# New due-date shifts and load lags in the list scheduler of a fused pooled-attention and MLP kernel

## The chip, the cores and the metric

The kernel runs on one core of a Trainium2 chip. The metric is the device time of one execution in microseconds (us), as the median of several runs; lower is better.

## The reference

`q`, `k` and `v` have 8 batches, 8 heads, 576 tokens and 64 columns per head, in float32. Keys and values are summed over windows of 8 tokens first, so 576 queries meet 72 keys.

```python
k_p = k.reshape(B, H, Sp, pool, D).mean(axis=3)
v_p = v.reshape(B, H, Sp, pool, D).mean(axis=3)
scores = scale * np.matmul(q, k_p.transpose(0, 1, 3, 2))
attn = softmax(scores)            # exp(scores - max) / sum
x = matmul(attn, v_p)             # -> 4608 tokens x 512
h = x @ w_in                      # 512 -> 2048
g = h * (1.0 / (1.0 + np.exp(-1.702 * h)))
out = g @ w_out                   # 2048 -> 512
```

## The kernel before

**Stages.** The weights `w_in` and `w_out` are loaded once, decoded and kept on the chip as a high and a low part, so that one product becomes three matmuls of the fast 32-bit format: high x high, low x high, high x low. The 512 first tokens of each attention batch form one batch of the MLP (c = 0 to 7), and the 64 left-over tokens of all eight form the last one (c = 8). The attention of batch b runs on the other engines while TensorE (PE) does the products of the MLP batch before it. One batch of the MLP takes about 96 us of PE, and some 85 us pass at the start until the first weights are decoded and the first attention is done.

**Products.** Batches 0 and 1 do `x @ w_in` directly (function `dense`: line 1217 and the two behind it for h, 1259 to 1261 for o). From batch 2 on, two of the sixteen 128-wide blocks of the hidden width are a pair p (0 to 7), whose 2x2x2 blocks are done in seven products instead of eight, by sums of blocks of x and of the weights made ahead (function `pair`). A product is six matmuls of 256 columns at L1421. Four products of a pair go to a PSUM bank ha and three to a bank hb. Each product of ha is copied out by `keep` (L1436, ScalarE = ACT or VectorE = DVE) before the next may be added to the same bank; `plus` (L1443, DVE) adds hb to a copied part. Pair p+1 takes the two banks that pair p leaves, so its first product waits for the last copy of ha. After a part is complete comes the gelu (L1460 and L1468 on ACT, the difference at L1475 on GpSimd = POOL or DVE), which gives the operands ghall and glall of the second product: groups of three matmuls of 512 columns (L1622 to L1624), eight groups for each pair, into four accumulators oC_0, oC_128, oC_256 and oC_384 of batch C. A complete accumulator is copied by ACT to a staging buffer osb with two places and stored from there (L1172; the third copy of a batch waits for the first one's store, the fourth for the second one's).

**The attention beside it.** For batch B, SP's queue loads keys and values in two halves (kvB_u_False the keys, kvB_u_True the values; function `fetch_main`, issued at L470, two DMAs of 128 KB for each half), queries in pieces (qr, L522, four DMAs a piece) and the tails of 64 tokens (tl). DVE sums the windows (L553: redB_v0 and redB_v1 are the values, red_k the keys; L563 spreads them with a mask), turns the queries (L740), takes the maximum of the scores sps (L779, L787), and after the exponentials on ACT (L799) the sum, the inverse and the product (L804, L816, L817, L822 on sm and sc), and copies the weights of the attention to main and tail (L851, L861, DVE or ACT). Scores are matmuls at L756; the transposes of the weights at L880 (apt) and the product with the values at L958 (pav) are PE's too. In the batches up to 2, main and tail are written by L822 directly. The first operands of a pair of batch C come back from DRAM through SP: wsC_p_0 to wsC_p_2 (512 KB each) and the last one in a place named shared (256 KB; L1354, function `fetch_pair`).

**What sets the order.** The program is written down as tasks, and a list scheduler, class `Plan`, decides in which order each engine gets its instructions. A task has a kind, made of the engine, what it writes and its batch and part ("DVE red2_0", "PE o1_128"), and a due time: where none is given, it is worked back from the tasks that need it, as their due time less SLACK times (duration + lag). Then SHIFTS adds a number for the task's kind. `wait` tells how long after a task another may begin that needs it: for a DMA its lag (2.2 us unless LAGS gives another), 0.25 or 1.2 us for PE, else 0.2. `order` goes through a modelled time and gives each engine that is free the ready task with the earliest due time. The instructions are emitted in the order so planned. On the chip each engine works through its own list in that order, and waits for semaphores where an operand is late; modelled times don't delay anything there. DMAs are issued by SP in list order too, so a DMA that waits for its buffer holds up those behind it. The operands of a pair go to the places of the pair two before it: the load of shared for pair 2 waits for the last product of pair 0 that reads it, ha5_0's fourth, and that of ws5_3_1 for hb5_1's second product.

Of the kernel before, what the change touches and what calls it, by code (L numbers as in the profile page):

```python
# [19 lines left out]
POOL = 8  # L20
# [4 lines left out]
EAGER = 50.0  # L25
UNTIL = 58.0
WARM = 222.0
SLACK = 1.5
BLOCKED = 20.0

LAGS = {"kv": 3.2, "tl": 3.0, "qr": 2.5}

SHIFTS = {
    "ACT g0_256": 14, "ACT g1_0": 8, "ACT gh0_0": -4, "ACT gh0_256": -8, "ACT gh1_0": -33, "ACT osb0_128": 17,
    "ACT qt0_1": 2, "ACT stage": 13, "ACT vh0": 6, "ACT x0_0": 12, "ACT x1_0": 18, "ACT x2_0": -18, "DMA qr2_0": -12,
# [5 lines left out]
    "POOL raw": 18, "POOL stage": 2, "POOL stage0_2": -22, "POOL stage0_6": -9, "POOL stage0_7": -49,  # L43
}


# [22 lines left out]

class Task:  # L70
    __slots__ = "engine us emit due after before bufs ready left begun table k port other mode kind lag".split()


class Plan:
# [54 lines left out]
    @staticmethod  # L129
    def wait(a, b):  # L130

        if a.engine == b.engine and a.engine != "DMA":
            return 0.0
        if a.engine == "DMA":
            return a.lag
        if b.engine == "OUT":
            return 2.2
        if b.engine == "PE":
            return 0.25 if b.due < 150 else 1.2
        return 0.2  # L140

    def room(self, t, wanted):
        need = {}
# [12 lines left out]
    def order(self):  # L156
# [2 lines left out]
            if t.due is None:  # L159
                t.due = min([o.due - SLACK * (t.us + self.wait(t, o)) for o in t.after] + [LATEST])  # L160
        for t in self.tasks:
            t.due += SHIFTS.get(t.kind, 0.0)
        free = dict.fromkeys(ENGINES, 0.0)
        free["DMA"] = 2.0
        port = {"DVE": 0.0, "POOL": 0.0}
# [24 lines left out]
        while len(placed) < len(self.tasks) or running:  # L190
            for end, k, t in sorted(running):
                if end > now + 1e-9:
                    break
                running.remove((end, k, t))
                for b in t.bufs:
                    b.users -= 1
                    if not b.users and b.ring is not None:
                        b.ring.room += 1
                for o in t.after:
                    o.left -= 1  # L200
                    o.ready = max(o.ready, end + self.wait(t, o))
                    if not o.left:
                        offer(o)
            for e in ENGINES:
                if free[e] > now + 1e-9:
                    continue
                rival = {"DVE": "POOL", "POOL": "DVE"}.get(e)
                blocked = rival is not None and port[rival] > now
                best = None
                for t in ready[e]:  # L210
                    if t.ready > now + 1e-9 or e != t.engine and now < t.due:
                        continue
                    rank = (t.due + (BLOCKED if blocked and t.port and e == "DVE" else 0.0), t.k)
                    if (best is None or rank < best[0]) and self.room(t, wanted):
                        best = rank, t
                if best is None:
                    continue
                t = best[1]
                ready[t.engine].remove(t)
                us = t.us  # L220
                if t.other is not None:
                    ready[t.other[0]].remove(t)
                    if e != t.engine:
                        t.engine, us, t.emit, t.port = t.other
                if t.table not in (None, table):
                    table, us = t.table, us + 1.28
                if e == "PE":
                    if now < COLD:
                        us *= 2.0
                    elif t.mode != mode:  # L230
                        us += 0.08
                    mode = t.mode
                if e == "DMA" and now < 16:
                    us *= 1.25
                if t.port:
                    if blocked:
                        us += port[rival] - now
                    port[e] = now + us
                for b in t.bufs:
                    if b.ring is not None and not b.held:  # L240
                        b.held = True
                        b.ring.room -= 1
                        if b.ring.fifo:
                            b.ring.queue.pop(0)
                t.begun, t.us, free[e] = now, us, now + us
                running.append((now + us, t.k, t))
                placed.append(t)
            times = [end for end, _, _ in running]
            times += [f for f in free.values() if f > now + 1e-9]
            times += [t.ready for e in ENGINES for t in ready[e] if t.ready > now + 1e-9]  # L250
            times += [t.due for e in ENGINES for t in ready[e] if t.other is not None and t.due > now + 1e-9]
            if not times:
                if len(placed) < len(self.tasks):
                    raise RuntimeError(f"stuck at {now}")
                break
            now = min(times)
# [4 lines left out]
def attention_moe_kernel(ctx: ExitStack, tc: tile.TileContext, q, k, v, w_in, w_out, out):  # L261
# [1081 lines left out]
    def fetch_pair(c, p):  # L1343

        got = []
        for k in range(4):
            if k < 3:
                b, also = home(2 * W_PLACES[p % 2][k], [P, 2, 512], F32R, f"ws{c}_{p}_{k}"), []
            else:
                b, whole = share(LAST_PLACE, [P, 2, 2, 256], F32R, p % 2, f"ws{c}_{p}_{k}")  # L1350
                also = [whole]
            t = dma(
                P * (4096 if k < 3 else 2048),
                lambda b=b, k=k: nc.sync.dma_start(out=b().bitcast(F32), in_=w_dram[p][k]),  # L1354
                [w_refs[p][k]],
                [b],
            )
            hold(t, *also)
            got.append(b)

        def op(k, half):
            cols = slice(256 * half, 256 * half + 256)
            return got[k], lambda: got[k]()[:, :, cols].rearrange("p r (j c) -> p r j c", j=2)

        return {"11": op(0, 0), "12": op(0, 1), "s3": op(1, 0), "s1": op(1, 1), "s2": op(2, 0), "s4": op(2, 1), "22": op(3, 0)}
# [191 lines left out]
    for b in range(1, B):  # L1557
# [17 lines left out]
        if b == FROM - 1:  # L1575
            stage = quarters([P, 2, CHUNK], F32, "stage")
# [108 lines left out]
```

## Time and profile before

| | |
|---|---|
| median of three runs | 930.7 us (928.47, 930.70, 934.69) |
| the profiled execution | 930.27 us |
| its span, first to last instruction | 928.2 us |
| PE busy with matmuls | 908.7 us, 98% |
| PE's weight loads | 813.3 us, 88% |
| DVE / ACT / POOL busy | 71% / 59% / 34% |
| granted clock of PE | 1.00 |

A row of a timeline gives start, length, engine, line, operation, what is written and read, and in brackets the idle time before it and who ended that. Batch and buffer numbers are left out of the names there. A row of waits gives who waited for whom, and then the sum, the number and the longest. DVE and ACT are idle for large parts, but they work in order, so a late operand of one instruction delays all that is behind it.

### The profile page before, as it was taken

To read this page: it belongs to the slowest core of one execution; us is meant where nothing else is said; L and a number is where in the kernel's file an instruction comes from. 1 tells how busy PE (TensorE), PEld (TensorE's weight loads), DVE (VectorE), ACT (ScalarE), POOL (GpSimd) and SP (SyncE) were. 2 spreads that over 40 slices of the span, in tenths; PEclk is the share of its full clock that TensorE was granted. 3 is DMA by queue.
4 is the path that set the end of the run, shared out by engine and by line. 5 is a ranking of instruction groups with operands and counts; after the bars stand their busy time and mean duration, and the time that the engine had idled before them with its cause. 6 is when DMAs were issued, how large, how long until landed. Compare 5 with 4: busy or idle time off the path is not lost.

```text
span 928.2 us, 16289 instructions
## 1 busy us (share of the span) xinstructions
PE 908.7 (98%) x5689; PEld 813.3 (88%) x5689; DVE 657.4 (71%) x1232; ACT 545.5 (59%) x1211; POOL 318.8 (34%) x306
## 2 busy tenths in 40 slices
PE   9999999999999999999999999999999999999997
PEld 9887988888889889898889898889988988999986
DVE  4989988787788875878778886888797743333222
ACT  3777755353448764766566865676577663334443
POOL 0666831888252251213522251226122460000000
PEclk9999999999999999999999999999999999999999
DMA  9993423554657478756785589558964575556541
GB/s 261 379 378 107 130 70 88 163 165 173 206 131 223 137 228 224 233 159 189 211 254 155 183 228 264 155 166 231 267 180 150 169 255 164 178 177 225 177 137 46
DMA packets 145265, 176.71 MB, mean 190 GB/s; under 512 B 85664, under 2 KB 96928, under 8 KB 145184
## 3 DMA queue, kind: packets, MB, share of 16 engines
q1 hardware_dynamic: 140336, 166.89, 60.3%
q10 hardware_dynamic: 4848, 8.78, 2.7%
q8 instruction: 45, 0.74, 0.3%
q14 instruction: 36, 0.29, 0.1%
HBM read 150.47 MB, written 25.17 MB: 189 GB/s over the span
## 4 chain that ended last, share of the span: by engine, by line
PE 76%; DMA 8%; DVE 7%; SPq 3%; ACT 2%; issue 2%; ACTq 0%; DVEq 0%
PE ha L1421 14%; PE hb L1421 11%; PE o L1624 9%; PE o L1623 9%; PE o L1622 9%; PE sps L756 3%; DMA raw<-in_moe_w_out_dram 3%; PE h L1217 3%; PE h L1219 3%; PE h L1218 3%; PE o L1260 2%; PE o L1259 2%; PE o L1261 2%; DMA ws<-wd 2%; DMA kv_True<-in_v_dram 1%
## 5 line engine op out<-in xcount | busy, mean ns | idle before, releaser
L1624 PE MATMUL o<-w,glall 128*128 128x512 f32 x448 | 176.5, 394 | 0.0
L1622 PE MATMUL o<-w,ghall 128*128 128x512 f32 x448 | 176.2, 393 | 0.0
L1623 PE MATMUL o<-w,ghall 128*128 128x512 f32 x448 | 175.8, 392 | 0.0
L1475 POOL TENSOR_TENSOR glall<-shared,ghall 128x256 fp32r<-128x256 f32 x91 | 74.5, 819 | 233.9 <-ACT shared L1468 176.1
L1421 PE MATMUL hb<-x,ws 128*128 128x256 f32 x672 | 99.0, 285 | 2.0 <-DVE gall L1443 1.4
L1624 PEld LDWEIGHTS o<-w,glall 128*128 128x128 f32 x448 | 84.2, 188 | 18.5
L1421 PEld LDWEIGHTS ha<-xs,ws 128*128 128x128 f32 x672 | 93.3, 189 | 7.1 <-ACT shared L1436 0.3
L1421 PE MATMUL ha<-xs,ws 128*128 128x256 f32 x672 | 98.9, 283 | 0.0
L1421 PEld LDWEIGHTS hb<-x,ws 128*128 128x128 f32 x672 | 89.6, 189 | 8.9 <-DVE shared L1443 3.5
L1460 ACT ACTIVATE ghall<-shared 128x256 fp32r<-128x256 f32 x150 | 62.6, 417 | 51.7 <-DVE shared L1443 35.5
L1622 PEld LDWEIGHTS o<-w,ghall 128*128 128x128 f32 x448 | 84.6, 189 | 9.1
L1623 PEld LDWEIGHTS o<-w,ghall 128*128 128x128 f32 x448 | 84.1, 188 | 9.3
L1443 DVE TENSOR_TENSOR shared<-shared,hb 128x256 f32<-128x256 f32 x112 | 46.4, 414 | 54.6 <-PE hb L1421 36.6
L1436 ACT COPY shared<-ha 128x256 f32<-128x256 f32 x103 | 38.2, 371 | 73.0 <-PE ha L1421 71.2
L1468 ACT ACTIVATE shared<-shared 128x256 f32<-128x256 f32 x150 | 62.7, 418 | 4.8
L1217 PE MATMUL h<-x,w 128*128 128x256 f32 (+1 forms) x192 | 63.2, 329 | 2.0 <-DVE raw L1131 1.9
L1218 PE MATMUL h<-x,w 128*128 128x256 f32 (+1 forms) x192 | 61.2, 319 | 0.3 <-DVE w L1152 0.3
L1219 PE MATMUL h<-x,w 128*128 128x256 f32 (+1 forms) x192 | 61.1, 318 | 0.0
L1475 DVE TENSOR_TENSOR glall<-shared,ghall 128x256 fp32r<-128x256 f32 x59 | 29.8, 505 | 41.8 <-ACT shared L1468 40.4
L1475 POOL TENSOR_TENSOR glall<-gall,ghall 128x256 fp32r<-128x256 f32 x37 | 29.9, 810 | 83.4 <-ACT gall L1468 62.8
L1421 PE MATMUL ha<-x,ws 128*128 128x256 f32 x336 | 51.0, 287 | 3.7 <-DVE shared L1436 1.8
L1247 POOL TENSOR_TENSOR gl<-g,gh 128x512 fp32r<-128x512 f32 x27 | 36.4, 1349 | 52.1 <-ACT gh L1239 50.3
(176 smaller groups left out, 2122.5 us busy)
## 6 DMA issues: line engine op xcount, KB each, us to landing
ws<-wd SPq DMA_DIRECT2D x168, 512.0 KB
shared<-wd SPq DMA_DIRECT2D x56, 256.0 KB
out_dram<-osb ACTq DMA_DIRECT2D x32, 256.0 KB
wd<-stage SPq DMA_DIRECT2D x16, 512.0 KB
raw<-in_moe_w_in_dram SPq DMA_DIRECT2D x15, 512.0 KB
raw<-in_moe_w_out_dram SPq DMA_DIRECT2D x15, 512.0 KB
kv_False<-in_k_dram SPq DMA_DIRECT2D x28, 256.0 KB
kv_True<-in_v_dram SPq DMA_DIRECT2D x28, 256.0 KB
```

What stands on the lines that cost most here:

```text
L1217: nc.tensor.matmul(o, lhsT=w[:, 0, j], rhs=xs[:, 0], start=j == 0, stop=False)
L1218: nc.tensor.matmul(o, lhsT=w[:, 1, j], rhs=xs[:, 0], start=False, stop=False)
L1219: nc.tensor.matmul(o, lhsT=w[:, 0, j], rhs=xs[:, 1], start=False, stop=j == NJ - 1)
L1421: nc.tensor.matmul(o, lhsT=wv()[:, r, jj], rhs=xo(k, jj), start=start and n == 0, stop=n == len(terms) - 1,  skip_group_check=not start,)
L1436: t = copy(256, lambda copy: copy(out=part(i), in_=bank()[:, 0:256]), [bank], [at(i)])
L1443: lambda: nc.vector.tensor_tensor(out=part(i), in0=part(i), in1=hb()[:, half * 256 : half * 256 + 256], op=ALU.add),
L1460: lambda: nc.scalar.activation(out=gh(), in_=src(), func=AF.Gelu_apprx_sigmoid),
L1468: lambda: nc.scalar.activation(out=part(i), in_=src(), func=AF.Gelu_apprx_sigmoid),
L1475: engine.tensor_tensor(out=gl(), in0=part(i), in1=gh().bitcast(F32), op=ALU.subtract)
L1622: nc.tensor.matmul(o(), lhsT=gh()[:, tok], rhs=w()[:, 0], start=start, stop=False)
L1623: nc.tensor.matmul(o(), lhsT=gh()[:, tok], rhs=w()[:, 1], start=False, stop=False)
L1624: nc.tensor.matmul(o(), lhsT=gl()[:, tok], rhs=w()[:, 0], start=False, stop=stop)
```

## The change

All numbers of the scheduler are replaced, and some that were fixed become parameters. The lag of the loads of keys and values goes from 3.2 to 5.1 us, of the tails from 3.0 to 5.5, of the queries from 2.5 to 3.8; the weights' operands of a pair get 1.06 where 2.2 was the default. SLACK falls from 1.5 to 1.07, the lag in front of PE from 1.2 to 0.95, and POOL's durations count 8.6% longer. The table SHIFTS has 116 entries instead of 49, nearly all with other values. A kind whose batch is written n ("DVE redn_0") holds for every batch from 3 on; the new function `later` makes that name. What is computed stays the same.

```diff
-SLACK = 1.5
+SLACK = 1.06861
...
-LAGS = {"kv": 3.2, "tl": 3.0, "qr": 2.5}
+LAGS = {"kv": 5.09777, "tl": 5.4771, "qr": 3.81139, "ws": 1.05954}
+WAITS = {"early": 0.241397, "PE": 0.951726, "other": 0.212011}
+COSTS = {"DVE": 1.00019, "ACT": 1.00325, "POOL": 1.08587}
...
 SHIFTS = {
...
-    "DVE raw": -6, "DVE sm1_0": -35, "DVE sm1_1": 10, "DVE tail2_0": 14, "DVE vbd1": 19, "PE h0_0": 1, "PE h1_0": 3,
...
+    "DMA kv1_0": 29.2, "DMA kvn_0": -6.3, "DMA qr2_0": -5.8, "DMA qrn_0": -18,
...
+    "DVE qtn_1": 115.6, "DVE raw": -45.1, "DVE red2_0": 17.4, "DVE redn_0": -24.5, "DVE redn_1": -17.5,
...
+    "PE kpsn_0": 4.7, "PE o0_0": 15.7, "PE o0_128": 11.2, "PE o1_0": -17.3, "PE o1_128": -20.8, "PE o1_256": -18.1,
...
 }
...
+def later(kind):
+
+    name = re.sub("^([^0-9]*)[3-9](?![0-9])", r"\1n", kind)
+    return name if name != kind else None
...
-            return 0.25 if b.due < 150 else 1.2
-        return 0.2
+            return WAITS["early" if b.due < 150 else "PE"]
+        return WAITS["other"]
...
-            t.due += SHIFTS.get(t.kind, 0.0)
+            t.due += SHIFTS.get(t.kind, 0.0) + SHIFTS.get(later(t.kind), 0.0)
...
+                us *= COSTS.get(e, 1.0)
...
                 lambda b=b, k=k: nc.sync.dma_start(out=b().bitcast(F32), in_=w_dram[p][k]),
                 [w_refs[p][k]],
                 [b],
+                lag=LAGS["ws"],
             )
```

Lines of the changed kernel lie 23 lower up to the first rows of `fetch_pair`, and 24 lower behind it. What the new numbers do to the order is seen at three places.

**SP, the values of batch 6.** DMAs in the order of SP's queue, before; kv6_1_True is the second half of the values:

```order
L522 DMA qr6_1_0_6538<-in_q_dram 32x10x32
L1354 DMA ws5_2_1_6547<-wd2_1_106 128x1024
L522 DMA qr6_1_0_6538<-in_q_dram 32x10x32 x3
L1354 DMA shared8_2533<-wd2_3_108 128x512
L522 DMA qr6_1_1_6591<-in_q_dram 32x10x32
L470 DMA kv6_1_True_6599<-in_v_dram 64x2x512 x2
L522 DMA qr6_1_1_6591<-in_q_dram 32x10x32
L1354 DMA ws5_2_2_6627<-wd2_2_107 128x1024
```

And in the change:

```order
L493 DMA kv6_0_True_6588<-in_v_dram 64x2x512 x2
L545 DMA qr6_1_0_6613<-in_q_dram 32x10x32 x4
L545 DMA qr6_1_1_6642<-in_q_dram 32x10x32 x4
L1377 DMA ws5_3_0_6664<-wd3_0_109 128x1024
L1377 DMA ws5_3_1_6678<-wd3_1_110 128x1024
L493 DMA kv6_1_True_6694<-in_v_dram 64x2x512 x2
L1377 DMA shared8_2539<-wd3_3_112 128x512
L1377 DMA ws5_3_2_6722<-wd3_2_111 128x1024
```

The half of the values stood between two pieces of queries, behind the operand shared of pair 2; it now stands behind the second operand of pair 3, and the queries that were spread over the queue go out in fours.

**DVE, the softmax of batch 6.** red6_v1 is the sum over that load, gall and shared12 are places for the parts of a pair. Before:

```order
L1436 COPY gall_3186<-ha5_1_6618 128x256
L553 TENSOR_REDUCE red6_v1_6658<-kv6_1_True_6599 128x128
L1443 TENSOR_TENSOR gall_3186<-gall_3186,hb5_1_6637 128x256
L804 TENSOR_REDUCE sm6_0_6680<-sc6_0_6545 128x16
L816 TENSOR_SCALAR sm6_0_6680<-sm6_0_6680 128x16
L817 RECIPROCAL sm6_0_6680<-sm6_0_6680 128x16
L822 TENSOR_TENSOR sc6_0_6545<-sc6_0_6545,sm6_0_6680 128x1152
L1443 TENSOR_TENSOR shared12_3019<-shared12_3019,hb5_1_6637 128x256
L851 COPY tail6_0_6717<-sc6_0_6545 32x2x32
L861 COPY main6_0_6720<-sc6_0_6545 32x2x4x32 x3
L851 COPY tail6_0_6717<-sc6_0_6545 32x2x32 x2
L1436 COPY shared12_3019<-ha5_1_6618 128x256
```

And in the change:

```order
L827 TENSOR_REDUCE sm6_0_6750<-sc6_0_6562 128x16
L1467 TENSOR_TENSOR shared12_2817<-shared12_2817,hb5_2_6730 128x256
L839 TENSOR_SCALAR sm6_0_6750<-sm6_0_6750 128x16
L840 RECIPROCAL sm6_0_6750<-sm6_0_6750 128x16
L845 TENSOR_TENSOR sc6_0_6562<-sc6_0_6562,sm6_0_6750 128x1152
L1499 TENSOR_TENSOR glall0_3055<-shared12_2817,ghall0_3037 128x256
L884 COPY main6_0_6793<-sc6_0_6562 32x2x4x32 x3
L1460 COPY gall_3163<-ha5_2_6681 128x256
L884 COPY main6_0_6793<-sc6_0_6562 32x2x4x32 x4
L874 COPY tail6_0_6836<-sc6_0_6562 32x2x32 x5
L576 TENSOR_REDUCE red6_v1_6851<-kv6_1_True_6694 128x128
L1467 TENSOR_TENSOR gall_3163<-gall_3163,hb5_2_6730 128x256
```

The sum of the values stood ahead of the softmax (L804 to L822) and now stands behind it and behind the copies to main and tail. A copy of ha5_1 stood behind the softmax and most of its copies; now it is one of ha5_2 that stands among them.

**PE, the end of batch 5.** The last groups of the accumulators o5 and the first products of batch 6, before:

```order
L1421 MATMUL ha6_0_7604<-x6_7532,shared8_2533 128x256 x6
L1622 MATMUL o5_256_6683<-w1_14_1584,ghall1_3149 128x512
L1623 MATMUL o5_256_6683<-w1_14_1584,ghall1_3149 128x512
L1624 MATMUL o5_256_6683<-w1_14_1584,glall1_3164 128x512
L1622 MATMUL o5_384_6690<-w1_14_1584,ghall1_3149 128x512
L1623 MATMUL o5_384_6690<-w1_14_1584,ghall1_3149 128x512
L1624 MATMUL o5_384_6690<-w1_14_1584,glall1_3164 128x512
L756 MATMUL sps7_0_2_7746<-k27_7614,qt7_0_2_7716 128x144 x2
L756 MATMUL sps7_0_3_7749<-k27_7614,qt7_0_3_7726 128x144 x2
L1421 MATMUL hb6_0_7625<-xs6_3_7414,ws6_0_2_7491 128x256 x6
L1421 MATMUL ha6_1_7768<-x6_6928,ws6_1_0_7507 128x256 x6
```

And in the change:

```order
L1648 MATMUL o5_256_6689<-w1_14_1543,glall1_3144 128x512
L779 MATMUL sps7_0_0_7685<-k27_7673,qt7_0_0_7394 128x144 x2
L779 MATMUL sps7_0_1_7688<-k27_7673,qt7_0_1_7478 128x144 x2
L1445 MATMUL ha6_0_7596<-x6_7553,shared8_2539 128x256 x6
L1445 MATMUL hb6_0_7612<-xs6_3_7439,ws6_0_2_7458 128x256 x6
L1445 MATMUL ha6_1_7716<-x6_6984,ws6_1_0_7506 128x256 x6
L1646 MATMUL o5_128_6725<-w1_14_1543,ghall0_3037 128x512
L1647 MATMUL o5_128_6725<-w1_14_1543,ghall0_3037 128x512
L1648 MATMUL o5_128_6725<-w1_14_1543,glall0_3055 128x512
L1646 MATMUL o6_384_7732<-w1_1_458,ghall1_3121 128x512
L1647 MATMUL o6_384_7732<-w1_1_458,ghall1_3121 128x512
L1648 MATMUL o6_384_7732<-w1_1_458,glall1_3144 128x512
```

Before, the accumulators o5_256 and o5_384 end one behind the other, with the scores of batch 7 behind them, and hb6_0 between them and ha6_1. In the change o5_256 ends ahead of the scores, o5_128 comes last, behind ha6_1's first product, and a group of batch 6 (o6_384) stands behind the last but one group of o5_128, whose last group follows on these rows; ha6_0's last product and ha6_1's first have one product of hb6_0 between them.

More of the change, by code (lines that the diff above doesn't have):

```diff
@@ L27 @@
 WARM = 222.0
-SLACK = 1.5
+SLACK = 1.06861
 BLOCKED = 20.0
-LAGS = {"kv": 3.2, "tl": 3.0, "qr": 2.5}
+LAGS = {"kv": 5.09777, "tl": 5.4771, "qr": 3.81139, "ws": 1.05954}
+WAITS = {"early": 0.241397, "PE": 0.951726, "other": 0.212011}
+COSTS = {"DVE": 1.00019, "ACT": 1.00325, "POOL": 1.08587}
 SHIFTS = {
-    "ACT g0_256": 14, "ACT g1_0": 8, "ACT gh0_0": -4, "ACT gh0_256": -8, "ACT gh1_0": -33, "ACT osb0_128": 17,
-    "ACT qt0_1": 2, "ACT stage": 13, "ACT vh0": 6, "ACT x0_0": 12, "ACT x1_0": 18, "ACT x2_0": -18, "DMA qr2_0": -12,
[5 rows of a table removed]
-    "POOL raw": 18, "POOL stage": 2, "POOL stage0_2": -22, "POOL stage0_6": -9, "POOL stage0_7": -49,
[3 rows of a table added]
+    "ACT sc1_0": 53.9, "ACT sc1_1": 26.5, "ACT stage": 19.2, "ACT tailn_0": -24, "ACT tailn_1": -28.1,
[4 rows of a table added]
+    "DVE csn_2": 16.9, "DVE e": 6.4, "DVE kbd2": 55.7, "DVE kbdn": -3.4, "DVE main0_0": 5.5, "DVE mtn_0": 82.7,
+    "DVE nm0_1": 6.9, "DVE nm2_0": 21, "DVE nm2_1": 20.3, "DVE nmn_0": -82.9, "DVE qt1_0": -1.4, "DVE qtn_0": 13.9,
+    "DVE qtn_1": 115.6, "DVE raw": -45.1, "DVE red2_0": 17.4, "DVE redn_0": -24.5, "DVE redn_1": -17.5,
[11 rows of a table added]
 }
```

21 rows, old and new, of the table SHIFTS are left out of this document.

## The prediction

> **What bounds the kernel now.** I read the page first, then the busy time by stretch of time, then TensorE's waits, then the chain of waits behind single ones.
>
> ```profile
> span 928.2 us, 16289 instructions
> PE 908.7 (98%) x5689; PEld 813.3 (88%) x5689; DVE 657.4 (71%) x1232; ACT 545.5 (59%) x1211; POOL 318.8 (34%) x306
> ```
>
> TensorE (PE) is busy for 98% of the span, so no other engine can be the bound. Whatever the order of the work does, it does through the 19.5 us in which PE stands still. The table by stretch (columns: stretch, its length, PE busy, weight loads, DVE, ACT, POOL, clock, DMA share, GB/s) says where these are:
>
> ```profile
> 0.00:80.00 80.00, 74.56 (x535) 68.27 (x535) 62.43 (x105) 51.52 (x101) 39.23 (x39) 1.00 0.93 309
> 80.00:134.00 54.00, 51.27 (x351) 46.31 (x351) 48.92 (x77) 40.15 (x73) 39.10 (x33) 1.00 0.39 108
> 326.00:710.00 384.00, 378.43 (x2409) 341.16 (x2408) 300.44 (x597) 249.32 (x583) 115.21 (x126) 1.00 0.71 205
> 806.00:902.00 96.00, 96.00 (x600) 86.64 (x599) 29.61 (x72) 42.10 (x106) 0.00 (x0) 1.00 0.57 179
> 902.00:929.00 27.00, 21.18 (x122) 18.26 (x120) 7.14 (x16) 9.17 (x23) 0.00 (x0) 0.98 0.15 39
> ```
>
> Length less PE gives 8.2 us of standstill up to 134 us, 5.6 us from 326 to 710, nothing from 806 to 902 (there no attention runs beside the products), and 5.8 us in the tail, where the last rows are copied and stored. The tail has no place to shrink. So the change can win some 14 us at the very most (19.5 - 5.8), 1.5% of the time. The waits from 230 to 806 us by who ended them (sum, times, longest):
>
> ```profile
> PE ha L1421 <- DVE shared L1436: 1.8, 3, 0.9
> PE hb L1421 <- DVE gall L1443: 1.4, 2, 1.2
> PE ha L1421 <- DVE gall L1436: 0.9, 1, 0.9
> PE ha L1421 <- ACT shared L1436: 0.8, 1, 0.8
> PE apt L880 <- DVE at L908: 0.3, 1, 0.3
> PE hb L1421 <- DVE shared L1443: 0.3, 1, 0.3
> ```
>
> These are the copies that empty a bank (L1436) and the sums that do the same (L1443): short work that came late. Why late is seen at batch 6, on DVE (start, length, what, and in brackets the idle time before and what ended it) and on PE:
>
> ```profile
> 573.64 2.01 DVE L553 TENSOR_REDUCE red_v<-kv_True 128x128 f32<-128x1024 f32 x1 [1.71 <-DMA kv_True<-in_v_dram]
> 578.25 1.36 DVE L822 TENSOR_TENSOR sc<-sc,sm 128x1152 f32<-128x1152 f32 x1
> 581.38 0.42 DVE L1436 COPY shared<-ha 128x256 f32<-128x256 f32 x1
> ```
>
> ```profile
> 568.38 0.40 PE L1624 MATMUL o<-w,glall 128*128 128x512 f32 x1
> 568.61 0.87 PE L1421 MATMUL hb<-xs,ws 128*128 128x256 f32 x6
> 569.32 0.88 PE L1421 MATMUL ha<-x,ws 128*128 128x256 f32 x6
> 580.60 0.88 PE L1421 MATMUL hb<-xs,ws 128*128 128x256 f32 x6
> 581.86 0.97 PE L1421 MATMUL ha<-x,ws 128*128 128x256 f32 x6 [0.38 <-DVE shared L1436]
> 582.99 1.69 PE L1421 MATMUL hb<-x,ws 128*128 128x256 f32 x12 [0.16 <-DVE gall L1443]
> ```
>
> DVE works in order. It stood 1.71 us in front of the sum of the values (red_v), whose load had not landed; the softmax behind it was late by that much, and so was the copy that empties ha's bank. Where nothing waits (568.38 to 569.32), a matmul of an output group is followed after 0.23 us and a product (six matmuls of 256 columns) after 0.71, so ha would have begun at 581.31 instead of 581.86: 0.55 us lost where the profile shows 0.38. Each wait costs some 0.16 us more than its idle time.
>
> The same load is behind the waits of batches 4 and 5, a load of keys (kv_False) behind that at 437.90, and a store behind that at 676.91. PE's rows for these four:
>
> ```profile
> 387.94 0.98 PE L1421 MATMUL ha<-x,ws 128*128 128x256 f32 x6 [0.93 <-DVE shared L1436]
> 437.90 0.39 PE L1421 MATMUL hb<-x,ws 128*128 128x256 f32 x1 [1.25 <-DVE gall L1443]
> 486.13 0.98 PE L1421 MATMUL ha<-x,ws 128*128 128x256 f32 x6 [0.91 <-DVE gall L1436]
> 676.91 0.97 PE L1421 MATMUL ha<-x,ws 128*128 128x256 f32 x6 [0.79 <-ACT shared L1436]
> ```
>
> How long the loads and the store took from their issue is in the chain of waits:
>
> ```profile
> 427.92 7.64 DMA kv_False<-in_k_dram
> ...
> 568.62 4.92 DMA kv_True<-in_v_dram
> ...
> 661.34 5.99 DMA out_dram<-osb
> ```
>
> **The change part by part.** It adds no arithmetic: PE has the same products and one warming matmul more. It moves instructions. Three moves carry the forecast; they stand in the section on the change.
>
> *Loads of values and keys.* Before, kv6_1_True goes out behind the load that waits for ha5_0's fourth product, and red6_v1 stands on DVE right behind the copy of ha5_1, past hb5_0's third sum. On PE lie between the two: two output groups (three matmuls of 0.23 us, 0.69 each), two pairs of scores (0.98 by the matmuls' spacing in the same view) and one product (0.71), 3.1 us in all. The load took 4.92 us: DVE must wait, and does. In the change the load goes out behind ws5_3_1, which waits for hb5_1's second product; red6_v1 stands behind hb5_2's first sum, with four products, four output groups and two pairs of scores between (2.8 + 2.8 + 1.0 = 6.6 us), and besides behind the softmax and its copies, which were behind it before. So it is covered for a load of 4.92 and nearly for one of 7.64, and a late one no longer delays the softmax. The first load of keys, which DVE awaited at 435, goes out in two halves far apart and has some 10 us of PE's work before its sum.
>
> By the fit in the Trainium skill (DMA: Bandwidth & Descriptors, "Anatomy of one DMA"), about 2 us plus the bytes at 436 GB/s, 256 KB would take 2.6 us by estimate; then 3.1 us would have covered it and this move would win nothing. The row of 4.92 us and DVE's wait say otherwise, for a queue that has weights ahead.
>
> *Stores.* The output buffer osb has two places, so ACT's third and fourth copy of a batch wait until the first and second store have landed:
>
> ```profile
> 667.41 0.59 ACT L1172 COPY osb<-o 128x512 f32<-128x512 f32 x1 [3.05 <-DMA out_dram<-osb]
> 669.30 1.28 ACT L799 ACT_TABLE_LOAD   x1
> 670.60 1.17 ACT L799 ACTIVATE sc<-sc 128x1152 f32<-128x1152 f32 x1
> 676.50 0.36 ACT L1436 COPY shared<-ha 128x256 f32<-128x256 f32 x1
> ```
>
> Here the exponentials behind the copy were late, and then the copy of ha. Before, the fourth block of batch 5 (o5_384) is complete 3.5 us of PE's work after the second; in the change the fourth (o5_128) is complete 8.0 us after the second, against 5.99 us for a store. The third stays at 5 to 6 us after the first, a wait of under 1 us on ACT, which has 30% to spare.
>
> Price of both: the waits with rows above, 0.93 + 1.25 + 0.91 + 0.38 + 0.16 + 0.79 = 4.4 us, with 0.16 for each of six 5.4 us. I take 4.5 of them, since a copy that is no longer 1 us late can still be 0.2 late. Bounds: nothing, and all of the six rows by waits, 5.5 + 9 x 0.16 = 6.9 us.
>
> *The start.* PE's waits up to 134 us that have a decoder or an attention step behind them:
>
> ```profile
> PE apt L880 <- DVE main L822: 1.9, 2, 1.1
> PE h L1217 <- DVE raw L1131: 1.9, 1, 1.9
> PE pav L958 <- ACT left L1005: 0.8, 1, 0.8
> ```
>
> The shift of DVE's decode steps (raw) goes from -6 to -45.1, so they get precedence in the new list, so a bank that a weight is decoded in is given back sooner; the second row is a wait for such a bank. Against it, the first weights' softmax product (main0_0) moves behind the tail's product and three short steps on DVE, which can lengthen the first row. I take 1.0 us of gain, half of the second row. Bounds: the three rows gone, 4.6 us, or the first row doubled with the rest kept, 1.9 us of loss.
>
> *What it costs.* The new list packs PE tighter: in batches 4 to 6 the first product of pair 1 follows ha's fourth product of pair 0 with one product between, 0.71 us, where batch 6 had some 3 us before (two output groups, the scores, a product). The copy that lies between took 0.36 us on ACT (the row of 676.50). By the order, 24 fewer instructions stand on DVE and 37 more on ACT, which runs at 59%. I put 0.5 us for copies that come a little late; bounds 0 and 2.6 us (five batches, each late by a copy of 0.36 and 0.16).
>
> Sum: -4.5 - 1.0 + 0.5 = -5.0 us. The profiled execution took 930.27 us (2.1 us more than its span) and lies 0.4 us under the median of the three runs, 930.7. 930.27 - 5.0 = **925.3 us**.
>
> **The rivals.** (1) *More comes of it: the start tightens too.* All 6.9 us of the middle go and 4.6 us of the start: 930.27 - 11.5 = 918.8. For it speaks that the three moves have one direction; against it that up to 80 us the DMA engines are 93% busy, which no order shortens.
>
> (2) *Nothing measurable: the waits move.* ha and hb have two banks for all products, and the tightest cover of a bank's emptying, one product of 0.71 us, is as tight in the change and more frequent (by the order 41 of the 110 turns of a bank from one pair to the next, 36 before). Copies late for whatever reason would wait there again; 4.5 us saved and 4 lost leave 929.8. Against it: from 806 to 902 us the same cover serves most turns, and PE stands still for 0.00 us, so it is enough when DVE and ACT are on time. The Trainium skill (Perfetto Trace Analysis, "Identifying Performance Opportunities") reads the same gap repeating as a sign of too few buffers, by which a reordering wins nothing; the stretch without attention bears it out only in part.
>
> (3) *Slower: the tight turns meet the exponentials.* Twice in each batch ACT loads a table and runs the exponentials, 1.28 + 1.17 = 2.45 us, and if a copy that empties a bank stands behind, PE waits for what 0.71 us does not cover: 2.45 + 0.36 + 0.16 - 0.71 = 2.3 us. With six batches and two each, all of them cost 27 us: 930.27 - 5.0 + 27 = 952; half of them, 939. From seven of twelve on, the kernel is slower by over 1%. For it: the turn with one product between, which now lies in the middle of the attention. Against it: the list can put the copy on the other engine, and DVE has the more copies at just these places.
>
> **How the numbers follow.** A change of 1%, 9.3 us, is about what a measurement of this kernel can tell from none: 921.4 and 940.0 us are the marks. The forecast (921.4 to 928) has 0.46, rival 1 (916 to 921.4) 0.28, rival 2 (928 to 934) 0.14, rival 3 0.12. Faster by over 1% is rival 1, 0.28; slower are the cases of rival 3 with seven turns or more, 0.10; the rest, 0.62, is within 1%. The range leaves out the bottom of rival 1 and rival 3: 917 to 934.
>
> **What would show it.** Right: DVE's waits in front of red_v and red_k, now
>
> ```profile
> DVE red_v L553 <- DMA kv_True<-in_v_dram: 8.1, 5, 2.7
> DVE red_k L553 <- DMA kv_False<-in_k_dram: 3.3, 2, 2.2
> ```
>
> fall under 3 us together; ACT's wait of 3.05 us for a store is gone; PE's standstill from 326 to 710 us is under 2 us instead of 5.6, and ha waits for no L1436 over 0.5 us. The forecast is wrong if the first two come true and the standstill stays (rival 2), if ha's waits name ACT with an exponential before them (rival 3), or if the stretch up to 134 us changes by more than 3 us either way, which I hold for less likely than not.

## The result and the profile after

The changed kernel takes 922.46 us (median of five runs, 920.73 to 924.86), before 930.70 (928.47 to 935.78): a ratio of 0.990, with a 95% interval of 0.986 to 0.994. The forecast was 925.3. The profiled execution of the change is the slowest of its five, 924.86 us; against before's 930.27 it shows 5.4 us of the 8.2. Page and stretches of the change (stretch, its length, PE busy, weight loads, DVE, ACT, POOL, clock, DMA share, GB/s):

```profile
span 923.1 us, 16292 instructions
PE 907.4 (98%) x5691; PEld 814.0 (88%) x5691; DVE 640.6 (69%) x1208; ACT 550.8 (60%) x1248; POOL 315.9 (34%) x293
```

```profile
0.00:80.00 80.00, 76.61 (x563) 71.82 (x564) 61.50 (x110) 54.61 (x105) 43.41 (x40) 1.00 0.92 304
80.00:134.00 54.00, 53.69 (x374) 49.45 (x373) 44.24 (x77) 38.16 (x69) 38.40 (x33) 1.00 0.42 115
134.00:326.00 192.00, 190.54 (x1069) 164.94 (x1068) 148.99 (x248) 99.46 (x201) 92.54 (x81) 1.00 0.54 163
326.00:422.00 96.00, 91.85 (x578) 83.21 (x577) 72.95 (x148) 61.73 (x146) 24.57 (x27) 0.98 0.67 198
422.00:710.00 288.00, 287.37 (x1842) 260.13 (x1841) 235.31 (x457) 193.00 (x473) 88.45 (x90) 1.00 0.72 209
```

Three stretches of before that the prediction does not show by themselves:

```profile
134.00:326.00 192.00, 191.36 (x1081) 166.15 (x1080) 158.38 (x260) 100.89 (x205) 95.12 (x84) 1.00 0.52 158
326.00:422.00 96.00, 94.47 (x602) 85.22 (x601) 71.09 (x142) 58.73 (x139) 28.72 (x31) 1.00 0.70 202
422.00:710.00 288.00, 283.96 (x1808) 255.95 (x1807) 229.35 (x456) 190.60 (x445) 86.49 (x95) 1.00 0.72 206
```

Length less PE is PE's standstill. It falls from 8.2 to 3.7 us up to 134 us and from 4.0 to 0.6 from 422 to 710, and it rises from 1.5 to 4.2 between 326 and 422 and from 0.6 to 1.5 ahead of that. So the change has a good start, a bad stretch from 326 to 422 us, where batch 2 of the MLP ends, and a good one behind it. The waits of PE in the change, up to 134 us:

```profile
PE warm L1609 <- POOL ident masks.py:199: 1.4, 1, 1.4
PE tpt L903 <- DVE tail L845: 1.1, 1, 1.1
PE apt L903 <- DVE main L845: 0.8, 1, 0.8
PE apt L903 <- DVE al L969: 0.3, 1, 0.3
```

Before has there, besides the three rows of the prediction, the same 1.4 us of warm, two rows of 0.3 and 0.2 us for h, and these:

```profile
PE apt L880 <- DVE at L908: 0.6, 1, 0.6
PE qps L728 <- DVE at L908: 0.4, 1, 0.4
PE tpt L880 <- DVE al L946: 0.4, 1, 0.4
```

From 326 to 422, the bad stretch, three waits make up all of the change's standstill:

```profile
PE ha L1445 <- ACT gall L1460: 2.2, 1, 2.2
PE hb L1445 <- DVE shared L1467: 1.5, 1, 1.5
PE hb L1445 <- ACT shared L1460: 0.5, 1, 0.5
```

The first is a store, on ACT's timeline (start, length, what, and the idle time before with what ended it) and in the chain of waits:

```profile
364.67 0.59 ACT L1195 COPY osb<-o 128x512 f32<-128x512 f32 x1
369.46 0.58 ACT L1195 COPY osb<-o 128x512 f32<-128x512 f32 x1 [2.79 <-DMA out_dram<-osb]
370.51 0.37 ACT L1460 COPY gall<-ha 128x256 f32<-128x256 f32 x1 [0.47 <-ACT osb L1195]
```

```profile
362.49 6.89 DMA out_dram<-osb
```

The third copy of batch 2 stood 2.79 us on ACT until the first store had landed, and the copy of ha stood behind it. In batches 3 to 6 of the change no copy to osb waits for a store. PE's wait behind that copy cost more than its 2.2 us, because the granted clock was halved behind it. First PE's rows, then the stretch of the slow ones with its clock (columns as above):

```profile
370.93 1.52 PE L1445 MATMUL ha<-x,ws 128*128 128x256 f32 x6 [2.18 <-ACT gall L1460]
372.25 1.48 PE L1445 MATMUL hb<-xs,ws 128*128 128x256 f32 x6
376.06 0.88 PE L1445 MATMUL ha<-xs,ws 128*128 128x256 f32 x6
```

```profile
371.20:374.40 3.20, 3.20 (x15) 3.01 (x15) 2.46 (x5) 0.98 (x3) 0.73 (x1) 0.50 0.15 57
```

Two products took 1.52 and 1.48 us instead of 0.88; the clock was at 0.50 for 3.4 us in all (371.1 to 374.5), which is 1.7 us of work lost and is counted as busy time, not as standstill. Before's profile has no such place ahead of its last microsecond.

The second wait is DVE's work beside the same batch. Ahead of the sum that empties hb stand 2.04 us of copies to main (six in a row in the profile's timeline, 332.57 to 334.61), 0.46 us of waiting for ACT and a transpose of 0.51 us.

### The profile page after: what moved, and what is told of

Same layout as the page of the kernel before. It is cut to its first block, busy times and chain, and to the rows that moved or that the text cites. A ratio compares the mean times of both kernels' runs of the same rounds, so it can differ in the third digit from the quotient of the medians.

```text
span 923.1 us, 16292 instructions
## 1 busy us (share of the span) xinstructions
PE 907.4 (98%) x5691; PEld 814.0 (88%) x5691; DVE 640.6 (69%) x1208; ACT 550.8 (60%) x1248; POOL 315.9 (34%) x293
## 4 chain that ended last, share of the span: by engine, by line
PE 87%; DVE 5%; DMA 3%; ACT 2%; issue 1%; SPq 0%; ACTq 0%; POOL 0%; DVEq 0%; POOLq 0%
PE ha L1445 16%; PE hb L1445 12%; PE o L1647 10%; PE o L1648 10%; PE o L1646 10%; PE sps L779 4%; PE h L1240 3%; PE h L1242 3%; PE h L1241 3%; PE o L1283 3%; PE o L1282 3%; PE o L1284 3%; PE warm L1609 1%; DVE main L884 1%; DMA out_dram<-osb 1%
## 5 line engine op out<-in xcount | busy, mean ns | idle before, releaser
L1499 POOL TENSOR_TENSOR glall<-shared,ghall 128x256 fp32r<-128x256 f32 x79 | 71.0, 902 | 247.2 <-ACT shared L1492 126.4
L1648 PEld LDWEIGHTS o<-w,glall 128*128 128x128 f32 x448 | 84.4, 188 | 19.5 <-POOL glall L1499 1.1
L1445 PE MATMUL hb<-x,ws 128*128 128x256 f32 x672 | 96.8, 285 | 3.0 <-DVE shared L1467 1.9
L1460 ACT COPY shared<-ha 128x256 f32<-128x256 f32 x116 | 42.9, 370 | 82.1 <-PE ha L1445 79.9
L1499 POOL TENSOR_TENSOR glall<-gall,ghall 128x256 fp32r<-128x256 f32 x40 | 34.2, 859 | 119.3 <-ACT gall L1492 86.9
L1499 DVE TENSOR_TENSOR glall<-shared,ghall 128x256 fp32r<-128x256 f32 x71 | 36.3, 512 | 43.0 <-ACT shared L1492 39.3
L1445 PEld LDWEIGHTS ha<-x,ws 128*128 128x128 f32 x336 | 44.9, 191 | 6.1 <-ACT gall L1460 3.1
```

What stands on the lines that cost most here:

```text
L1445: nc.tensor.matmul(o, lhsT=wv()[:, r, jj], rhs=xo(k, jj), start=start and n == 0, stop=n == len(terms) - 1,  skip_group_check=not start,)
L1460: t = copy(256, lambda copy: copy(out=part(i), in_=bank()[:, 0:256]), [bank], [at(i)])
L1499: engine.tensor_tensor(out=gl(), in0=part(i), in1=gh().bitcast(F32), op=ALU.subtract)
L1648: nc.tensor.matmul(o(), lhsT=gl()[:, tok], rhs=w()[:, 0], start=False, stop=stop)
```

## The experiments

Each ran five rounds against before on the same chip; before was 930.4 to 931.3 us there. The list of tasks with their engines, as the scheduler plans it, can be written out and replayed, so that two orders are joined at a planned time or one task is moved with nothing else changed:

```diff
+ORDER = (
...
-    order = plan.order()
+    order = plan.replay()
```

`replay` emits the tasks in the order of the list. Below, a diff shows how the list is made. Line numbers of these kernels lie some 50 to 150 higher; names are the same.

**The change's order in stretches.** First its start alone.

```diff
-ORDER = before
+ORDER = change[:203 us] + before[rest]
```

> The change's order up to the last products of the first MLP batch (the first 203 us of its plan), the order of before behind it; nothing else differs. By the two profiles the changed kernel has the same useful matmuls behind it 6.6 us earlier at 200 us of the run. Theory (each stretch of the order has its own gain, and they add): 930.7 - 6.6 = 924, and PE's standstill up to 134 us falls from 8.2 to about 2 us. Rival (what the start gains is waited away again in the middle, where loads and stores set the pace): 929 to 931, with longer waits from 326 to 710 us.

Measured: 924.54 us, ratio 0.9935 (0.9912 to 0.9959). PE's busy time is 76.61 us of the first 80 and 53.69 of the next 54, the change's own rows to the hundredth. The start alone brings about 6 us, six times what I had put. The rest is the late part:

```diff
-ORDER = before
+ORDER = before[:420 us] + change[rest]
```

> The order of before up to 420 us of its plan, the change's order behind it. By the two profiles the useful matmuls of the changed kernel gain 4.1 us from there to the end (1.2 us ahead at 419 us, 5.3 at the end). Theory (the moved loads and stores are what the middle gains): 930.7 - 4.1 = 926.6, DVE's waits in front of red_v and ACT's for a store gone behind 440 us. Rival (the gains of the middle come only with the start that goes with them): within 1 us of before.

Measured: 925.96 us, ratio 0.9944 (0.9925 to 0.9962), 5.2 us. PE's waits from 422 to 710 us of this kernel are one row:

```profile
PE hb L1572 <- DVE shared L1594: 0.4, 2, 0.2
```

where before's same stretch has five rows with 3.8 us together. So batches 3 to 6 gain with before's start too. What lies between:

```diff
-ORDER = before
+ORDER = before[:205 us] + change[205:423 us] + before[rest]
```

> The change's order only in between: before's up to 205 us of the plan, the change's up to 423 us, before's again behind it. In the two profiles the changed kernel loses 5.3 us of its lead in this stretch, in batch 2, by a wait behind a store of 6.89 us and one behind copies on DVE. Theory (this stretch of the new order is worse than the old one): 930.7 + 3 to 5 = 934 to 936, with waits of 2 us and 1.5 us at the same places. Rival (a chance of that one execution, which was the slowest of five): within 1 us of before and no wait of over 1 us there.

Measured: 938.05 us, ratio 1.0079 (1.0050 to 1.0108), slower by some 7 us. Most of it is no property of the change. At the joint to before's order PE waits 3.9 us (below), and behind that the clock is at 0.50 for 3.4 us (from 430.0), together 5.6 of the 8.1 us by which this profile's span exceeds before's; another 3.4 us at 0.50, worth 1.7, lie at 30.6 us, in before's own part of the order. The change's own three places show again:

```profile
PE hb L1573 <- DVE shared L1595: 1.1, 1, 1.1
PE ha L1573 <- ACT gall L1588: 0.6, 1, 0.6
PE hb L1573 <- ACT shared L1588: 0.5, 1, 0.5
```

2.2 us instead of 4.2 with the same order of this stretch. The wait behind DVE's copies belongs to the order; of the one behind the store, for which ACT stands 1.21 us here instead of 2.79, most does not. (In e7 below, which has the change's order of these stores too, the third copy waits for no store.) With the middle taken from before:

```diff
-ORDER = change
+ORDER = change[:203 us] + before[:420 us] + change[rest]
```

> The change's order with the stretch between taken from before: new up to 203 us, old up to 420, new behind it. Theory (stretches add): 930.7 - 6.6 - 4.1 = 920, faster than the change's 922.5 by what its middle costs. Rival (the loss in batch 2 was chance): 921 to 923, as the change. Rival (stretches don't add): slower than both single ones, over 924.

Measured: 921.46 us, ratio 0.9899 (0.9876 to 0.9921); the change has 0.990 (0.986 to 0.994). It is not told apart from the change. The parts add up only roughly: 0.65 and 0.56% make 1.21, measured 1.01. At the joint at 203 us the profile shows PE standing still for 2.6 us from 134 to 326 us, where the change has 1.5 and before 0.6, so I joined earlier:

```diff
-ORDER = change[:203 us] + before[:420 us] + change[rest]
+ORDER = change[:136 us] + before[:420 us] + change[rest]
```

> As the order with the middle of before, but the change's start goes only up to 136 us of the plan, since the seam at 203 us cost 2 us in the profile (PE's standstill from 134 to 230 us 3.2 us there, 1.2 in before). Theory (the seam cost them): 921.5 - 1.5 = 920. Rival (the loss sits in the middle order itself behind an earlier start): 921 to 922.

Measured: 923.66 us, ratio 0.9928 (0.9903 to 0.9954). The expectation failed: this joint is not the cheaper one. It has waits for DVE of 1.4 us ahead of the attention's products with the values (pav) and 0.6 us ahead of scores, all within 16 us behind it. A joint is an edit of its own.

**The start.** One shift of it, alone and taken out.

```diff
-    "DVE raw": -6,
+    "DVE raw": -45.1,
...
-ORDER = before
+ORDER = this[:142 us] + before[rest]
```

> Before, with only DVE's shift of the decode steps (raw) at -45.1 instead of -6 up to 142 us of the plan, and before's order behind it. Theory (the forecast's: the bank that a weight is decoded in comes back sooner): PE's wait of 1.9 us for DVE raw at 90 us is gone, 930.7 - 2 = 928.7. Rival (the start's gain of 6.6 us has another cause, the order of output groups, products and attention steps): the wait stays or another takes its place, 930 to 932.

Measured: 930.79 us, ratio 1.0004 (0.9985 to 1.0024). The wait at 90 us is gone, and PE is busier by 1.95 us from 80 to 134 us, but stands 1.32 us more from 40 to 80, where the product of x and w_in now waits 0.7 us for ACT's step of the gelu (gh) and 0.5 us for raw. Columns as above, first this kernel, then before:

```profile
40.00:80.00 40.00, 36.66 (x248) 32.69 (x248) 34.71 (x56) 33.13 (x64) 31.08 (x26) 1.00 0.84 303
80.00:134.00 54.00, 53.22 (x367) 48.62 (x366) 43.48 (x76) 36.98 (x66) 37.21 (x31) 1.00 0.40 113
```

```profile
40.00:80.00 40.00, 37.98 (x259) 34.15 (x257) 34.81 (x54) 30.40 (x60) 26.98 (x23) 1.00 0.87 311
```

Now the change's start without it:

```diff
-    "DVE raw": -45.1,
+    "DVE raw": -6,
...
-ORDER = change[:203 us] + before[rest]
+ORDER = this[:200 us] + before[rest]
```

> The change's numbers up to 200 us of the plan with one shift put back, DVE's decode steps (raw) at -6 instead of -45.1, and the order of before behind it; to be held against the run with the change's start alone, 924.5. Theory (the precedence of raw is needed, though alone it gave nothing): PE's waits for DVE raw between 60 and 134 us come back, 3 us slower, 927.5. Rival (the other shifts of the start bring the gain): 924 to 925.

Measured: 938.04 us, ratio 1.0079 (1.0051 to 1.0108), 13.5 us over the run with the whole start. The first row of PE's waits up to 134 us:

```profile
PE h L1369 <- DVE raw L1283: 6.0, 4, 1.8
```

Four products of x and w_in now stand for decode steps that come too late, and behind the third of these waits (at 75.9 us) the clock is at 0.50 for 3.4 us. The precedence is worth nothing alone, and without it the other shifts lose more than the start gains.

**Batches 3 to 7: the load, the sum, the store.** The sum of the values alone:

```diff
-DVE red6_1
 DVE sm6_0
...
+DVE red6_1
 DVE vbd6
```

> Before, with one thing moved in batches 3 to 7: DVE's sum over the second half of the values (red_v1) stands right ahead of the spread that needs it, behind the softmax and its copies in batches 4 to 6. The load is issued where it was. Theory (the late load held up the softmax and with it the copies of ha): DVE's wait of up to 2.7 us in front of red_v1 is gone, ha's waits at 388, 486 and 582 us (0.93, 0.91, 0.38) too, 930.7 - 2.7 = 928. Rival (the sum's 2 us on DVE make other copies late): 930 to 932, with waits of ha or hb some 10 us later.

Before has the sum ahead of the softmax in batches 4 to 6 only, so three sums moved. Measured: 931.20 us, ratio 1.0014 (0.9999 to 1.0030). The three waits of ha that I had laid to it are gone, and three new ones stand 10 us behind, where the product of the attention with the values (pav) waits for ACT, which is late by the sum:

```profile
PE pav L1110 <- ACT ghall L1612: 2.4, 3, 0.8
```

So a late sum did hold up the copies of ha, and what their waits cost is given back. In the change, where the load moved as well, pav waits once from 230 to 806 us, for 0.5 us. With the store's copy moved as well:

```diff
-ACT osb5_384
 ACT sc7_0
+ACT osb5_384
```

> As the run with the sum behind the softmax, and on ACT the fourth copy to osb of batches 3 to 5 moved behind the exponentials that it stood ahead of. Theory (ACT's wait for the first stores held up the exponentials, the softmax and a copy of ha): ACT's wait of 3.05 us for a store is under 1 us and ha's wait at 677 us (0.79) is gone, 1 us faster than without it, 927. Rival (the copy, now later, holds the accumulator's bank, and the next batch's fourth output group waits): the wait goes to PE's o, 930 or more.

Measured: 930.50 us, ratio 1.0011 (0.9993 to 1.0029). The longest wait of ACT for a store is 1.4 us instead of 3.0, but ha still waits for ACT at the same turn:

```profile
673.99 0.88 PE L1573 MATMUL hb<-xs,ws 128*128 128x256 f32 x6
676.03 0.98 PE L1573 MATMUL ha<-x,ws 128*128 128x256 f32 x6 [1.16 <-ACT shared L1588]
```

```profile
671.34 1.28 ACT L1612 ACT_TABLE_LOAD   x1
672.63 0.42 ACT L1612 ACTIVATE ghall<-shared 128x256 fp32r<-128x256 f32 x1
674.79 0.50 ACT L1003 COPY tail<-sc 32x64 f32<-32x64 f32 x2 [0.34 <-DVE sc L974]
675.62 0.36 ACT L1588 COPY shared<-ha 128x256 f32<-128x256 f32 x1
```

ACT's copy of ha stands behind copies of the softmax, which DVE (its sum at 668.2 first, then sm and sc) hands over late. The store was not what set that wait. The edit the other way, in the change and in five batches, 3 to 7, where before has it in three:

```diff
+DVE red6_1
 DVE sm6_0
...
-DVE red6_1
 DVE vbd6
```

> The change, with one thing put back in batches 3 to 7: red_v1 stands ahead of the softmax's first step, as before; the load is issued where the change has it, some 4.5 us of the plan ahead. Theory: DVE waits in front of red_v1 again, the softmax and copies behind it are late, ha's waits of 0.4 to 0.9 us come back in batches 4 to 6: 922.5 + 2.7 = 925. Rival (the sum's place is nothing, what gains is the rest of the order): within 1 us of the change, 921.5 to 923.5.

Measured: 945.38 us, ratio 1.0168 (1.0145 to 1.0191), 23 us over the change instead of 2.7. Waits of DVE and of PE from 230 to 806 us:

```profile
DVE red_v L704 <- DMA kv_True<-in_v_dram: 13.9, 6, 4.8
```

```profile
PE ha L1572 <- DVE gall L1594: 6.1, 1, 6.1
PE o L1775 <- DVE glall L1626: 4.7, 4, 1.9
PE hb L1572 <- DVE shared L1587: 2.6, 3, 0.9
```

DVE stands up to 4.8 us at the sum, and what is queued behind it are the differences that the output groups wait for and the copies of both banks. At the sum of batch 3 alone PE loses 6.1 us. PE's standstill is 27.6 us (span 942.0, PE busy 914.4), 11.9 more than in the change, about the 12.6 by which DVE stands longer in front of red_v (13.9 for 1.3). Another 6.8 us are the clock: it was at 0.50 for 17.1 us (from 290.6, 403.2, 597.8 and 696.8) instead of 3.4. Together that is 18.7 of the 18.9 us between the two profiled executions. The lags alone, and all but the lags:

```diff
-LAGS = {"kv": 3.2, "tl": 3.0, "qr": 2.5}
+LAGS = {"kv": 5.09777, "tl": 5.4771, "qr": 3.81139, "ws": 1.05954}
...
+                lag=LAGS["ws"],
```

> Before, with only the four lags of loads changed (keys and values 5.1, tails 5.5, queries 3.8, a pair's operands 1.06). In batches 4 to 6 the sum of the values is planned 6.6 us behind its load where before plans 4.7, still ahead of the softmax, and the last two store copies are as close as before. Theory (cover for the loads is half of what the middle gains, the sum's place and the stores the other half): DVE's waits in front of red_v fall from 8.1 us to under 4, 928 to 929. Rival (the lags are all of it): 925 to 926. Rival (the sum's new place is nothing and the new order packs worse): 931 or more.

Measured: 932.45 us, ratio 1.0023 (0.9999 to 1.0046). In the profiled execution DVE waits for no load of keys or values at all from 230 to 806 us, and from 326 to 710 us PE's standstill is 2.0 us:

```profile
326.00:422.00 96.00, 95.11 (x608) 86.00 (x608) 78.03 (x157) 63.56 (x147) 29.68 (x32) 1.00 0.72 206
422.00:710.00 288.00, 286.90 (x1833) 259.88 (x1832) 234.22 (x472) 190.74 (x440) 87.94 (x94) 1.00 0.71 206
```

That is 3.6 us less than before, with the sum still ahead of the softmax. In that execution it is lost at 232 us, where another order of DVE's work came with it:

```profile
PE pav L1008 <- DVE x L1039: 3.5, 1, 3.5
```

The chain there leads to a write of folded weights that took 6.41 us, and behind the wait the clock is at 0.50 for 3.4 us. The profiled execution, 928.26 us, is one of the four shortest of twelve; the other eight took 932.2 to 936.3 us, and no trace shows what they lost. The other way round:

```diff
-LAGS = {"kv": 5.09777, "tl": 5.4771, "qr": 3.81139, "ws": 1.05954}
+LAGS = {"kv": 3.2, "tl": 3.0, "qr": 2.5, "ws": 2.2}
```

> The change, with the lags of loads as before (3.2, 3.0, 2.5 and 2.2); shifts, SLACK, waits and costs are the change's. In batches 5 to 7 the sum of the values is planned 4.9 us behind its load and ahead of the softmax again, in batches 3 and 4 behind it. Theory (shifts and lags belong together: the tight order holds only where the sum is out of the way; putting the sum back by hand cost 23 us in five batches): 922.5 + 3 x 2.5 = 930, with DVE's waits in front of red_v in batches 5 to 7 and PE's waits for glall behind them. Rival (the shifts alone bring the gain): 922 to 924.

Measured: 936.60 us, ratio 1.0065 (1.0042 to 1.0088), 14 us over the change. DVE's waits from 230 to 806 us:

```profile
DVE red_v L670 <- DMA kv_True<-in_v_dram: 9.4, 8, 2.0
DVE red_k L670 <- DMA kv_False<-in_k_dram: 8.3, 6, 2.6
```

The shifts of the change without its lags are slower than before. The lag of 1.06 for the operands of a pair does nothing in the change: with 2.2 in its place the planned order is the same, row for row.

## Why the prediction was right

The sign and the time came out, 922.5 for 925.3 and within the range. Of the terms one held. Two were too small by some microseconds each, with opposite signs; that the sum came out as well as it did is in part luck.

- **What bounds it.** Right in the main. Of the 5.1 us that the profiled span lost, 3.8 are PE's standstill, 19.5 to 15.7 us, and 1.3 are busy time, 908.7 to 907.4, although the halved clock added 1.7 there. The 0.16 us that each wait costs beyond its idle time goes that way; no view here splits the busy time further.
- **The middle, -4.5 us.** Right in size for the place that I had looked at: from 422 us on, the order of the change alone gives 5.2 us (e2), and DVE's waits in front of red_v from 326 to 806 us fall from 8.1 to 0.5 us. The step "a late one no longer delays the softmax" was the lesser half. The sum behind the softmax gains nothing by itself (e5); more cover for the load removes the waits with the sum where it was (e9), and without the lags nothing holds (e10). That it is the cover rests on the waits in e9's profiled execution, whose median is no faster than before. The single prices did not hold either: the 0.79 us that I laid to the store stayed when the store's wait was cut (e6).
- **The loads' duration.** I took the row of 4.92 us. The runs agree with it: with the load planned 4.7 us ahead DVE waits, with 6.6 it does not (e9). The fit of the Trainium skill (DMA: Bandwidth & Descriptors, "Anatomy of one DMA"), which that section measured on DMAs issued by GpSimd, gives by estimate 2.6 us for one of the half's two transfers and 3.2 for both. These loads go out from SP beside others, and the trace's 4.92 us does not agree. (Each of the two has 256 KB by the profile's list of transfers; the section on the kernel says 128, which is wrong.)
- **The start, -1.0 us.** The step that failed: "half of the second row", bounded by 4.6 us. It gives about 6 (e1). I priced one shift by one wait. That shift alone gives nothing (e8), and the other shifts without it lose 7 us to before (e12); the gain belongs to them together. Most of the standstill up to 134 us goes with it, 8.2 to 3.7 us, the small waits too, and that is past the wait that I had priced. It came with the DMA engines as busy as before up to 80 us (0.92 and 0.93), which I had held against it.
- **What it costs, +0.5 us.** Too small: 3.4 us more standstill from 134 to 422 us in the profile. I had followed the order in batches 4 to 6, and batch 2 has shifts of its own: there the third copy to osb waited 2.79 us, where I had written under 1. With the same order of that stretch the three waits of 4.2 us were 2.2 in e3, and in e7 the two that are not behind the store were 2.0 and the one behind it was gone. So some 2 us belong to the order; the rest, and the halved clock behind it, came in the one execution that was traced, the slowest of five. A halved clock behind a long wait was in none of my terms.
- **The signs.** ACT's wait for stores went in batches 3 to 6 and stayed in batch 2 (2.79 us, before 2.13); ha waited 2.2 us once for a copy on ACT; standstill from 326 to 710 us fell to 4.8 us, not under 2; DVE's waits in front of red_v and red_k are 4.3 us together, not under 3, with 3.5 of them in one. Each failed between 326 and 422 us and held behind it. And the stretch up to 134 us changed by 4.5 us, which I had named as a sign against the forecast: the time came out with less from the middle and more from the start than I had written.
- **The rivals.** Rival 1, the start that tightens, came true by half: its start, not its middle. Rival 2 is what e5 did. Rival 3 was not seen in the change, but its chain was, at the joint of e3, where the exponentials and a table stood ahead of the copy of ha:

```profile
421.48 1.28 ACT L951
...
422.78 1.66 ACT sc L951
...
424.45 1.97 DVE sm L956
...
427.31 1.28 ACT L1612
...
429.47 0.27 ACT shared L1588
...
429.78 1.28 PE ha L1573 x5
```

There PE waited 3.9 us, where I had worked out 2.3: both tables, 1.28 us each, and DVE's sum of 1.97 us stood on the way. The Trainium skill (ScalarE: Activation LUTs, "What ACT_TABLE_LOAD costs") has about 1.28 us for the load and 1.38 for a drain with it. The trace agrees with the load; in e6's rows above it ends at 672.62 and the next instruction begins at 672.63, and the one ahead of it (670.70, 0.62 us long) ends 0.02 us before it begins, so no drain is seen there.

What stays open: which of the start's other shifts are needed beside raw's, why e4 gains 0.2% less than its parts (joints were only tried at two places behind the start), what eight of e9's twelve executions lost, and whether the four executions of the change that have no trace wait in batch 2 as the traced one does.

## What to carry to other kernels

Where engines work in fixed order, count for each load the work between its issue and its first use on the engine that waits, and compare that with the load's slow landings, not with its median or a formula: 4.7 us of planned cover left DVE waiting 8.1 us in front of red_v (before, 326 to 806 us), 6.6 us left no wait (e9). In this case waits that were removed by moving the waiting instruction were paid again by whoever needed its result (e5); those that were removed by an earlier issue were not, in the stretch where they lay (e9, 326 to 710 us). When a wait of TensorE is priced, look at the granted clock behind it, not only at the idle time. Entries of a table of precedences can't be priced one by one; look at every stretch that has entries of its own, and test a stretch by joining the old and the new order.

## What the runs showed of the hardware

- Transfers of 256 KB that ended a wait took 4.0 to 7.6 us from issue to landing beside other traffic (DMA share 0.7; 4.02, 4.92, 5.50 and 7.64 for loads, 5.99 and 6.89 for stores). The same store in the same order of its stretch held ACT for 2.79 us in the change, for 1.21 in e3 and not at all in e7.
- Behind some waits of PE the granted clock fell to 0.50 for 3.4 us, and products of 0.88 us took 1.5. It came behind waits of 2.18 (the change), 1.89 (e2, at 92 us), 2.81 (e10), 3.49 (e9) and 3.86 us (e3), once for twice as long at one of 6.13 (e7), and also behind shorter ones (e12, 1.45 at 75.9 us). It did not come behind before's wait of 1.86 us at the same place as e2's, nor behind e1's of 1.96 at 543 us or e12's of 1.84 at 121. What decides it no run here shows. By these figures each 3.4 us at 0.50 are 1.7 us of work lost. The two of e2's eleven executions with a mean clock of 0.996 took 927.45 and 927.67 us, the other nine 925.2 to 926.7 (0.997 to 1.000).
- One instruction of 2 us, moved ahead of its operand's landing in five batches, cost 23 us (e7). In the profiled executions it is 18.9 us: 11.9 of standstill of PE and 6.8 of halved clock.
